# Batch 0's last k tokens as fp32 through two hardware queues, and all sums of phi(k) ahead of v, in a linear-attention + MoE kernel

## The chip, the cores and the metric

The kernel runs on one core of one Trainium2 chip. Its time is device microseconds of one execution; 0.2% of it (about 0.58 us) is the least difference that counts here as a change. The profile is one execution recorded by the hardware profiler: PE is TensorE, DVE is VectorE, ACT is ScalarE, POOL is GpSimd, SP is SyncE. A name such as L212 is line 212 of the kernel before. DMAs can be issued from POOL (a software queue, which can turn fp32 into bf16 on the way) and from SP and ACT (hardware queues, which in this kernel copy without a cast).

## The reference

```python
def _attn_ref(q, k, v):              # (8, 8, 576, 64) = batch, heads, tokens, head_dim
    def phi(x):
        return np.where(x > 0, x, np.exp(x) - 1.0) + 1.0
    q_p, k_p = (phi(q), phi(k))
    kv = np.einsum('bhsd,bhse->bhde', k_p, v)
    z = np.sum(k_p, axis=2)
    num = np.einsum('bhsd,bhde->bhse', q_p, kv)
    den = np.einsum('bhsd,bhd->bhs', q_p, z)[..., None] + 1e-06
    return num / den

def _moe_ref(x, w_in, w_out, beta):  # x: 4608 x 512, w_in: 512 x 2048, w_out: 2048 x 512
    h = x @ w_in
    g = h * (1.0 / (1.0 + np.exp(-beta * h)))
    return g @ w_out
```

The attention output of each batch (576 tokens x 512) is the x of the second part. All tensors are fp32 in memory.

## The kernel before

The order of instructions on every engine is written out by hand (a manual schedule); semaphores between engines follow from the data. Matmuls are in bf16. PE does everything in one long sequence: for batch b it does the "h" phase (x times w_in, then Silu on ACT through `silu`, L467, which leaves g), and the "y" phase (g times w_out, L527), and the attention of batch b+1 is slipped in between these matmuls by the `plan` dictionaries. Phi is made of three instructions: `exp` on ACT, `relu` (max with 0, plus 1) on DVE, and `phi` (the minimum of both) on DVE. The scale by 1/beta is put into w_out by `w_out_scale` (L212 on DVE, L214 on ACT).

Batch 0 has its own code, since nothing can hide it: its 576 tokens are laid out as 64 partitions x 9 tokens (index j) for heads 0 to 3 (g = 0) and again 64 partitions x 9 for heads 4 to 7 (g = 1). Its loads are pieces (`load_nine`, L133, two DMAs each, one for each g): the last four tokens of each nine of k (`k_last`, fp32, j from KF = 5 to 8) by SP; the first five of k, the first four of q, v in two pieces and the rest of q by POOL, with cast; then w_in in four DMAs, w_out, and the next batches, all in POOL's queue. The row of beta comes through ACT's queue and is transposed by PE (`beta_trans`, L193) between two stretches of dummy matmuls (`warm`, L611), which are there while PE has no data.

The start of batch 0, then, in the order of each engine:

- ACT: `exp9` of the first five of k, of `k_last`, of q tokens 0-1 and 2-3 (all L266); the copy of the first transposed q out of PSUM (`q_out9`, L387), half of `kv_evac9` (L387, into `kv_bd`), the second `q_out9`, `exp9` of the rest of q, the copy of x transposed, the load of the Silu table (`silu_table`, L617), the first Silus.
- DVE: `relu9` (L274) of the first k, of `k_last`; `phi9` (L280) of the first k; `relu9` of q; `phi9` of `k_last`; `phi9` of q tokens 0-1 and 2-3; `make_beta` (five small instructions, L199 to L205); the other half of `kv_evac9` (L385); then `num_norm` (L435 to L437) of the first two token pairs.
- PE: `kv_mm0` (L325) four times: the sums of phi(k) over the first five tokens (moving operand: ones), the products with v of these, the sums of the last four, and, after the first `q_trans9` (L293), the products with v of the last four; then the second `q_trans9`, a `warm`, `num_mm` (L421) of the first two token pairs, four `warm`, and the transposes of x (`x_trans`, L455), upon which the h phase begins.

At the end of batch 0's h phase, while PE starts on `y_phase_wide(0)` (L527, four token tiles for each of ff = 0 to 11, then the rest), batch 1 is prepared. ACT takes exp of k (`exp_(1, 1)`) and of q (`exp_(1, 0)`, both L229). DVE takes the two `relu` (L237), `w_out_scale(2)` (four instructions, which wait for the DMAs of that part of w_out into `g`), `phi(1, 1)` for k, `phi(1, 0)` for q (L242), and a copy of v. `w_out_scale(2)` gives the weights of ff = 8 to 11. After ff = 10 PE transposes batch 1's q (`q_trans`, L395), which needs `phi(1, 0)`, and makes `kv_mm(1)` (L362); both take a buffer from the pool of two `att` buffers in PSUM, in this order.

Of the kernel before, what the change touches and what calls it, by code (L numbers as in the profile page):

```python
# [16 lines left out]
def kernel(  # L17
# [73 lines left out]
    def clear_tail(i):  # L91
        nc.vector.memset(xqk[i][TAIL:P, :, :, NJ, :], 0.0)
# [22 lines left out]
    N9 = S // TAIL  # L115

    def nine(a, spec):
# [10 lines left out]
    KF = 5  # L128
    k_last = g_f[:, 0 : HH * (N9 - KF) * D].rearrange(
        "p (h j d) -> p h j d", h=HH, j=N9 - KF  # L130
    )

    def load_nine(dst, src, j0, j1, eng=nc.gpsimd):  # L133
        for g in range(2):
            eng.dma_start(  # L135
                out=dst[g * TAIL : (g + 1) * TAIL].rearrange("p h j d -> p h (j d)"),
                in_=src[0, g * HH : (g + 1) * HH, :, :]
                .rearrange("h (p j) d -> p h j d", j=N9)[:, :, j0:j1, :]
                .rearrange("p h j d -> p h (j d)"),
            )  # L140

    small = consts.tile([P, 2], F32)
    nc.vector.memset(small, 0.0)
    nc.scalar.activation(small[:, 0:1], small[:, 0:1], ACTF.Exp)
    nc.vector.memset(g_sb[0][:, FC - 1, :], 0.0)  # L145
    load_nine(k_last, k, KF, N9, eng=nc.sync)
    clear_tail(1)
    nc.vector.memset(vraw[1][TAIL:P, :, NJ, :], 0.0)
    beta_row = consts.tile([FC, P], F32)
    nc.scalar.dma_start(out=beta_row, in_=moe_beta.rearrange("(c p) -> c p", p=P))  # L150

    identity = consts.tile([P, P], BF16)
    ident16 = consts.tile([FC, FC], F32)
# [37 lines left out]
    def beta_trans():  # L191
        st["bps"] = mm_bank([P, 512])[:, 0:FC]
        nc.tensor.matmul(  # L193
            st["bps"], beta_row, ident16, is_transpose=True, start=True, stop=True
        )
# [11 lines left out]
    def w_out_scale(i, on_dve=4):  # L207
        for c in range(4):
            ff = 4 * i + c
            dst, src, by = w_out_sb[i][:, c, :], w_out_f[i][c // 2][:, c % 2, :], rbeta[:, ff : ff + 1]  # L210
            if c < on_dve:
                nc.vector.tensor_scalar(dst, src, by, None, ALU.mult)  # L212
            else:
                nc.scalar.activation(dst, src, ACTF.Copy, scale=by)  # L214


    st = {}
# [16 lines left out]
    def relu(b, a, h0=0, h1=H):  # L234
        if h0 == 0:
            st[b, "r", a] = work.tile([P, H, NT, D], BF16, tag="r", name="r")
        nc.vector.tensor_scalar(  # L237
            st[b, "r", a][:, h0:h1], xqk[b % NX][:, a, h0:h1], 0.0, 1.0, ALU.max, ALU.add
        )

    def phi(b, a, h0=0, h1=H):
        nc.vector.tensor_tensor(  # L242
            st[b, "p"][:, a].rearrange("p j (h d) -> p h j d", h=H)[:, h0:h1],
            st[b, "r", a][:, h0:h1], st[b, "e", a][:, h0:h1], ALU.min,
        )
# [9 lines left out]
    def work9(tag, **kw):  # L255
        return nine(work.tile([P, H, NT, D], BF16, tag=tag, name=tag, **kw), "jhd")

    def in9(a, j0, j1):
        if a == 1 and j0 >= KF:
            return k_last[:, :, j0 - KF : j1 - KF]  # L260
        return x9[a][:, :, j0:j1]

    def exp9(a, j0, j1):
        if j0 == 0:
            st["e9", a] = work9("e", bufs=3)
        nc.scalar.activation(  # L266
            st["e9", a][:, j0:j1].rearrange("p j h d -> p h j d"), in9(a, j0, j1),
            ACTF.Exp,
        )

    def relu9(a, j0, j1):
        if j0 == 0:
            st["r9", a] = work9("r")
        nc.vector.tensor_scalar(  # L274
            st["r9", a][:, j0:j1].rearrange("p j h d -> p h j d"), in9(a, j0, j1),
            0.0, 1.0, ALU.max, ALU.add,
        )

    def phi9(a, j0, j1):
        nc.vector.tensor_tensor(  # L280
            st["p9"][a][:, j0:j1], st["r9", a][:, j0:j1], st["e9", a][:, j0:j1],
            ALU.min,
        )
# [29 lines left out]
    def kv_cols(kvp, g, a):  # L313
        m0 = a * 2 * (D + 1)
        return kvp[g][:, m0 : m0 + 2 * (D + 1)].rearrange("p (i e) -> p i e", i=2)

    def kv_mm0(kvp, j0, j1, of_v):


        for j in range(j0, j1):  # L320
            for a in range(2):
                for g in range(2):
                    gs = slice(g * TAIL, (g + 1) * TAIL)
                    cols = kv_cols(kvp, g, a)
                    nc.tensor.matmul(  # L325
                        cols[:, :, 0:D] if of_v else cols[:, :, D],
                        st["p9"][1][gs, j, 2 * a : 2 * a + 2, :],
                        v9[gs, 2 * a : 2 * a + 2, j, :] if of_v else ones[gs],
                        start=(j == 0 and a == 0 and not of_v),
                        stop=(j == N9 - 1 and a == 1 and of_v),  # L330
                        skip_group_check=True,
                    )
# [17 lines left out]
        )  # L350


    def kv_mm(b, p0=0, p1=KC):


        kvp = att_banks()[:, 0, 0 : KC * (D + 1)].rearrange("p (c e) -> p c e", c=KC)
        st[b, "kvp"] = kvp
        for p in range(p0, p1):
            for j in range(NT):
                for g in range(2):  # L360
                    c0 = p * P + g * D
                    nc.tensor.matmul(  # L362
                        kvp[g * D : (g + 1) * D, p, :],
                        st[b, "p"][:, 1, j, c0 : c0 + D],
                        vaug[b % 2][:, j, 2 * p + g, 0 : D + 1],
                        start=(j == 0), stop=(j == NT - 1), skip_group_check=True,
                    )
# [114 lines left out]
    def h_phase(b, x, groups, plan):  # L482
        for i, (ff, t0, t1) in enumerate(groups):
            hp = mm_bank([P, 512])
            h_mm(b, x, hp, ff, t0, t1)
            silu(b, ff, hp, t0 * P, t1 * P)
            run(plan, i)
# [121 lines left out]
    def warm(n):  # L609
        for _ in range(n):  # L610
            nc.tensor.matmul(  # L611
                st["warm"], g_sb[0][:, FC - 1, 0:P], g_sb[0][:, FC - 1, :],
                start=True, stop=True, skip_group_check=True,
            )
# [4 lines left out]
    def F(f, *a, **k):  # L619
        return lambda: f(*a, **k)  # L620
# [3 lines left out]
    warm(10)  # L624
    beta_trans()
    warm(15)
    exp9(1, 0, KF)
    exp9(1, KF, N9)
    exp9(0, 0, 2)
    exp9(0, 2, QF)  # L630
    relu9(1, 0, KF)
    relu9(1, KF, N9)
    phi9(1, 0, KF)
    relu9(0, 0, QF)
    phi9(1, KF, N9)
    phi9(0, 0, 2)
    phi9(0, 2, QF)
    make_beta()
    kvp = [mm_bank([P, 512]) for _ in range(2)]
    kv_mm0(kvp, 0, KF, False)  # L640
    kv_mm0(kvp, 0, KF, True)
    kv_mm0(kvp, KF, N9, False)
    qb = att_banks(BF16)
    q_trans9(0, qb, 0)
    q_out9(0, 1, qb, 0, False)
# [9 lines left out]
    num_norm(0, 1)  # L655
    exp9(0, QF, N9)
    relu9(0, QF, N9)
    warm(4)
    x_trans(0, 0)
    silu_table()  # L660
    x_trans(0, 1, dve=True)
# [13 lines left out]
    def q_rest():  # L675
        for t in range(2, NT):
            q_trans9(t, qb2, (t - 2) * 256)
        for t in range(2, NT):
# [24 lines left out]
    silu_table()  # L703
    relu(1, 1)
    relu(1, 0)
    w_out_scale(2)
    phi(1, 1)
    phi(1, 0)
    v_copy(1, 0, HH)
    v_copy(1, HH, H, dve=False)  # L710
    y_phase_wide(0, {
        4: [F(load_next, 3)],
        10: [
            F(q_trans, 1, 0, 1, 2, 3), F(kv_mm, 1), F(kv_evac, 1), F(w_out_scale, 3, 2),
        ],
        11: [F(num_mm, 1, 0), F(num_norm, 1, 0)],
        12: [F(num_mm, 1, 1), F(num_norm, 1, 1), F(x_trans, 1, 0, wide=True)],
# [20 lines left out]
    silu_table()  # L738
    y_phase_wide(1, {
        1: [F(phi, 2, 0), F(q_trans_dma, 2), F(phi, 2, 1)],  # L740
        6: [F(kv_mm, 2), F(kv_evac, 2)],
        8: [F(num_mm, 2, 0), F(num_norm, 2, 0)],
        9: [F(num_mm, 2, 1), F(num_norm, 2, 1)],
        10: [F(num_mm, 2, 2), F(num_norm, 2, 2)],
# [3 lines left out]
    for b in range(2, B + 1):  # L748
        n = b + 1
        groups = ALL  # L750
        plan = {}
        if b == 2:
            groups = (
                [(ff, 0, 2) for ff in range(8)] + [(ff, 2, 4) for ff in range(8)] + ALL[8:]
            )
        o = len(groups) - FC
        if n < B:
            plan[3 + o] = [F(relu, n, 0), F(phi, n, 0), F(q_trans_dma, n)]
            plan[5 + o] = [F(relu, n, 1), F(phi, n, 1)]
            plan[7 + o] = [F(v_copy, n), F(held_v, b + 3, n)]  # L760
            plan[12 + o] = [F(kv_mm, n)]
            plan[13 + o] = [F(kv_evac, n)]
        h_phase(b, xT[b % 3] if b < B else xT_tail, groups, plan)
        plan = {}
        if n + 1 < B:
            begin(n + 1)
            exp_(n + 1, 1)
            exp_(n + 1, 0)
        if n < B:
            for t in range(NT if n % 2 else NJ):  # L770
                plan[1 + 2 * t] = [F(num_mm, n, t)]
                plan[2 + 2 * t] = [F(num_norm, n, t)]
            plan[12] = [F(held_kq, b + 3, n)]
        y_phase(b, plan)
# [30 lines left out]
```

## Time and profile before

| | us |
|---|---|
| median of 5 runs (lowest, highest) | 291.71 (291.61, 291.73) |
| the profiled execution's own time | 291.72 |
| its span, first to last instruction | 289.8 |
| PE busy (97% of the span) | 281.5 |
| ACT busy (60%) | 174.0 |
| DVE busy (41%) | 118.0 |
| POOL busy (19%) | 53.8 |
| mean granted TensorE clock | 0.998 |

The profiled execution is 1.9 us longer than its span; that is time around the program which this change has no part in. PE is busy nearly always, so what matters is where it is not: the waits of PE, the stretch from 0 to 16 us in which its busy time is mostly `warm`, and the chain that leads to each wait. Times in the timeline are from the span's start. A timeline line can merge several instructions; "x4" at its end is their number, and the second column is the time from the first's start to the last's end. In square brackets stands the idle time before it and what ended it.

### The profile page before, as it was taken

How to read it: one execution, taken by the hardware profiler on the slowest of the kernel's cores; microseconds unless marked ns; L12 is line 12 of the kernel's file. 1: busy time of each engine (PE TensorE's matmuls, PEld its weight loads, DVE VectorE, ACT ScalarE, POOL GpSimd, SP SyncE). 2: the span in 40 equal slices, each digit the busy share in tenths (PEclk: the TensorE clock that was granted, in tenths of full speed). 3: DMA queues.
4: the chain of work that ended last, by engine and by line, in shares of the span. 5: the costliest groups of instructions: out<-in, count | busy, mean ns of one | idle time of the engine just before them, and what ended most of it. 6: DMA issues, size and time to landing. Idle time of an engine off the chain costs nothing.

```text
span 289.8 us, 4740 instructions
## 1 busy us (share of the span) xinstructions
PE 281.5 (97%) x1895; PEld 143.0 (49%) x1895; DVE 118.0 (41%) x235; ACT 174.0 (60%) x232; POOL 53.8 (19%) x79
## 2 busy tenths in 40 slices
PE   8889999999999999999999999999999999999994
PEld 3466445644576444454445444554455444444443
DVE  3874387504670365326532655173517300110012
ACT  2888788889998843875277617771850086017500
POOL 8923574300051204020402040000000000000000
PEclk9999999999999999999999999999999999999999
DMA  8999999999379977975794889333503500120033
GB/s 146 200 207 345 256 276 193 257 167 157 62 209 183 131 143 114 208 100 143 120 214 53 160 106 189 72 98 107 102 2 91 111 36 0 67 81 0 0 74 74
DMA packets 75766, 38.07 MB, mean 131 GB/s; under 512 B 43344, under 2 KB 70240, under 8 KB 75744
## 3 DMA queue, kind: packets, MB, share of 16 engines
q0 software_dynamic: 38912, 20.19, 49.0%
q1 hardware_dynamic: 36640, 17.44, 26.1%
q8 instruction: 15, 0.25, 0.4%
q10 hardware_dynamic: 192, 0.14, 0.2%
q14 instruction: 7, 0.06, 0.1%
HBM read 36.71 MB, written 9.44 MB: 159 GB/s over the span
## 4 chain that ended last, share of the span: by engine, by line
PE 83%; DMA 9%; POOL 4%; DVE 1%; ACT 1%; issue 1%; POOLq 0%; DVEq 0%
PE mm L527 38%; PE mm L475 37%; DMA xqk<-in_moe_w_out_dram 5%; DMA g<-in_moe_w_out_dram 4%; PE att L421 3%; PE att L362 2%; POOL xqk L135 1%; PE mm L558 1%; PE att L475 1%; POOL w_in L162 1%; DVE qk_p L242 1%; POOL vraw L135 1%; ACT q_pT L387 1%; PE att L395 0%; DVE w_out L212 0%
## 5 line engine op out<-in xcount | busy, mean ns | idle before, releaser
L467 ACT ACTIVATE g<-mm,beta_c 128x512 bf16<-128x512 f32 (+2 forms) x160 | 97.7, 623 | 86.2 <-PE mm L475 86.1
L527 PE MATMUL mm<-w_out,g 128*128 128x512 bf16 x560 | 128.0, 379 | 0.0
L475 PE MATMUL mm<-xT,w_in 128*128 128x512 bf16 (+2 forms) x576 | 107.5, 344 | 0.1
L475 PEld LDWEIGHTS <-w_in 128*128 128x128 bf16 x672 | 63.8, 98 | 59.4 <-DVE xT L385 0.4
L527 PEld LDWEIGHTS <-g 128*128 128x128 bf16 x560 | 53.1, 98 | 59.0 <-issue 0.3
L537 DVE COPY y_sb<-mm 128x512 f32<-128x512 f32 x27 | 18.7, 691 | 72.9 <-PE mm L527 69.4
L229 ACT ACTIVATE e<-xqk 128x2560 bf16<-128x2560 bf16 x14 | 31.9, 2329 | 0.1
L242 DVE TENSOR_TENSOR qk_p<-r,e 128x2560 bf16<-128x2560 bf16 x14 | 20.8, 1489 | 12.8 <-ACT e L229 12.2
L437 DVE TENSOR_TENSOR xs<-att,rden 128x512 bf16<-128x512 f32 x36 | 24.9, 691 | 1.2
L372 DVE CAST kv_bd<-att 64x260 bf16<-64x260 f32 x14 | 6.0, 427 | 35.9 <-PE att L362 35.8
L435 DVE TENSOR_SCALAR den<-att 128x8 f32<-128x8 f32 x36 | 5.8, 162 | 26.6 <-PE att L421 26.6
L421 PEld LDWEIGHTS <-q_pT 128*128 128x128 bf16 (+1 forms) x160 | 10.9, 100 | 9.5 <-issue 1.7
L421 PE MATMUL att<-kv_bd,q_pT 128*128 128x130 bf16 (+1 forms) x160 | 14.2, 222 | 0.7 <-DVE kv_bd L385 0.4
L475 PE MATMUL mm<-xT_tail,w_in 128*128 128x512 bf16 x64 | 14.0, 379 | 0.0
L594 POOL COPY held<-xT 1x1 bf16<-1x1 bf16 x4 | 2.0, 510 | 63.9 <-DMA xT<-xs 63.9
L237 DVE TENSOR_SCALAR r<-xqk 128x2560 bf16<-128x2560 bf16 x14 | 12.1, 871 | 3.9 <-DMA xqk<-in_q_dram 2.4
L611 PE MATMUL mm<-g 128*128 128x512 bf16 x30 | 9.1, 457 | 1.2 <-DVE g L145 1.2
L229 ACT ACT_TABLE_LOAD x7 | 9.0, 1283 | 0.1
L72 POOL DMA_DIRECT2D vraw<-in_v_dram x7 | 6.4, 910 | 9.6 <-DVE vaug L385 4.5
L72 POOL DMA_DIRECT2D xqk<-in_k_dram x7 | 7.1, 1021 | 4.5 <-DMA w_in<-in_moe_w_in_dram 1.6
L436 DVE RECIPROCAL rden<-den 128x8 f32<-128x8 f32 x36 | 7.3, 203 | 1.2
L475 PE MATMUL att<-xT,w_in 128*128 128x512 bf16 x32 | 7.2, 379 | 0.0
(77 smaller groups left out, 136.6 us busy)
## 6 DMA issues: line engine op xcount, KB each, us to landing
out_dram<-y_sb SPq DMA_DIRECT2D x28, 256.0 KB, 2.3
xqk<-in_k_dram POOLq DMA_DIRECT2D x7, 512.0 KB, 8.7
xqk<-in_q_dram POOLq DMA_DIRECT2D x7, 512.0 KB, 10.8
vraw<-in_v_dram POOLq DMA_DIRECT2D x7, 512.0 KB, 11.7
w_in<-in_moe_w_in_dram POOLq DMA_DIRECT2D x4, 512.0 KB, 10.2
g<-in_moe_w_out_dram POOLq DMA_DIRECT2D x4, 512.0 KB, 10.7
out_dram<-y_sb SPq DMA_DIRECT2D x14, 128.0 KB, 5.2
xqk<-in_moe_w_out_dram POOLq DMA_DIRECT2D x2, 512.0 KB, 14.3
```

The lines of the kernel that those rows point to most:

```text
L72: eng.dma_start(out=dst[:, :, 0:NJ, :].rearrange("p h j d -> p h (j d)"), in_=src[b, :, 0:MAIN, :].rearrange("h (p j) d -> p h (j d)", j=NJ),)
L229: nc.scalar.activation(st[b, "e", a][:, h0:h1], xqk[b % NX][:, a, h0:h1], ACTF.Exp)
L237: nc.vector.tensor_scalar(st[b, "r", a][:, h0:h1], xqk[b % NX][:, a, h0:h1], 0.0, 1.0, ALU.max, ALU.add)
L242: nc.vector.tensor_tensor(st[b, "p"][:, a].rearrange("p j (h d) -> p h j d", h=H)[:, h0:h1], st[b, "r", a][:, h0:h1], st[b, "e", a][:, h0: ...
L421: nc.tensor.matmul(nps[r0 : r0 + n, p // 2, c0 : c0 + 2 * (D + 1)], st[bb, "qT"][:, t, p, :n], kv_bd[bb % 2][:, p], start=True, stop=True, ...
L436: nc.vector.reciprocal(rden[:n], den[:n])
L437: nc.vector.tensor_mul(xs[:n], nv[:, :, :, 0:D], rden[:n, :, :, None].to_broadcast([n, 2, 4, D]))
L467: nc.scalar.activation(g_sb[b % 2][:, ff, c0:c1], hp[:, c0:c1], ACTF.Silu, scale=beta_c[:, ff : ff + 1],)
L475: nc.tensor.matmul(hp[:, c0:c1], w_in_sb[ff // 4][:, kc, (ff % 4) * P : (ff % 4 + 1) * P], x[:, t0:t1, kc, :] if b < B else x[:, kc, c0:c1 ...
L527: nc.tensor.matmul(yp, g_sb[b % 2][:, ff, t * P : (t + 1) * P], w_out_sb[ff // 4][:, ff % 4, :], start=(ff == 0), stop=(ff == FC - 1),)
L537: nc.vector.tensor_copy(y_sb, yp)
L611: nc.tensor.matmul(st["warm"], g_sb[0][:, FC - 1, 0:P], g_sb[0][:, FC - 1, :], start=True, stop=True, skip_group_check=True,)
```

## The change

Half of `k_last` (g = 0) is loaded by SP and half (g = 1) by ACT, both as the first thing that these engines do, ahead of ACT's load of the Exp table; beta's row goes to SP's queue, behind SP's half. On ACT and on DVE, `k_last` is worked on first: its exp, relu and phi stand ahead of those of the first five tokens of k. On PE the sums of phi(k) over all nine tokens are one run of 36 matmuls, ahead of all products with v. Two of the four `warm` between `num_mm` and the transposes of x are taken out. In the preparation of batch 1, `phi(1, 1)` stands ahead of `w_out_scale(2)` on DVE. The PSUM buffer of `kv_mm` is taken by a function of its own, `kv_bank`, which for batch 1 stands ahead of `q_trans`; for the other batches the order stays what it was.

```diff
-    def load_nine(dst, src, j0, j1, eng=nc.gpsimd):
-        for g in range(2):
+    def load_nine(dst, src, j0, j1, engs=(nc.gpsimd, nc.gpsimd)):
+        for g, eng in enumerate(engs):
             eng.dma_start(
...
     small = consts.tile([P, 2], F32)
+    load_nine(k_last, k, KF, N9, engs=(nc.sync, nc.scalar))
     nc.vector.memset(small, 0.0)
     nc.scalar.activation(small[:, 0:1], small[:, 0:1], ACTF.Exp)
     nc.vector.memset(g_sb[0][:, FC - 1, :], 0.0)
-    load_nine(k_last, k, KF, N9, eng=nc.sync)
...
-    nc.scalar.dma_start(out=beta_row, in_=moe_beta.rearrange("(c p) -> c p", p=P))
+    nc.sync.dma_start(out=beta_row, in_=moe_beta.rearrange("(c p) -> c p", p=P))
...
-    def kv_mm(b, p0=0, p1=KC):
-        kvp = att_banks()[:, 0, 0 : KC * (D + 1)].rearrange("p (c e) -> p c e", c=KC)
-        st[b, "kvp"] = kvp
-        for p in range(p0, p1):
+    def kv_bank(b):
+        st[b, "kvp"] = att_banks()[:, 0, 0 : KC * (D + 1)].rearrange(
+            "p (c e) -> p c e", c=KC
+        )
+
+    def kv_mm(b):
+        kvp = st[b, "kvp"]
+        for p in range(KC):
...
     warm(15)
+    exp9(1, KF, N9)
     exp9(1, 0, KF)
-    exp9(1, KF, N9)
     exp9(0, 0, 2)
     exp9(0, 2, QF)
+    relu9(1, KF, N9)
+    phi9(1, KF, N9)
     relu9(1, 0, KF)
-    relu9(1, KF, N9)
     phi9(1, 0, KF)
     relu9(0, 0, QF)
-    phi9(1, KF, N9)
     phi9(0, 0, 2)
     phi9(0, 2, QF)
     make_beta()
     kvp = [mm_bank([P, 512]) for _ in range(2)]
-    kv_mm0(kvp, 0, KF, False)
+    kv_mm0(kvp, 0, N9, False)
     kv_mm0(kvp, 0, KF, True)
-    kv_mm0(kvp, KF, N9, False)
     qb = att_banks(BF16)
     q_trans9(0, qb, 0)
...
-    warm(4)
+    warm(2)
     x_trans(0, 0)
...
     relu(1, 0)
+    phi(1, 1)
     w_out_scale(2)
-    phi(1, 1)
     phi(1, 0)
...
-            F(q_trans, 1, 0, 1, 2, 3), F(kv_mm, 1), F(kv_evac, 1), F(w_out_scale, 3, 2),
+            F(kv_bank, 1), F(q_trans, 1, 0, 1, 2, 3), F(kv_mm, 1), F(kv_evac, 1), F(w_out_scale, 3, 2),
```

More of the change, by code (lines that the diff above doesn't have):

```diff
@@ L263, in exp9 @@
     def exp9(a, j0, j1):
-        if j0 == 0:
+        if ("e9", a) not in st:
             st["e9", a] = work9("e", bufs=3)
@@ L271, in relu9 @@
     def relu9(a, j0, j1):
-        if j0 == 0:
+        if ("r9", a) not in st:
             st["r9", a] = work9("r")
@@ L740 @@
         1: [F(phi, 2, 0), F(q_trans_dma, 2), F(phi, 2, 1)],
-        6: [F(kv_mm, 2), F(kv_evac, 2)],
+        6: [F(kv_bank, 2), F(kv_mm, 2), F(kv_evac, 2)],
         8: [F(num_mm, 2, 0), F(num_norm, 2, 0)],
@@ L760 @@
             plan[7 + o] = [F(v_copy, n), F(held_v, b + 3, n)]
-            plan[12 + o] = [F(kv_mm, n)]
+            plan[12 + o] = [F(kv_bank, n), F(kv_mm, n)]
             plan[13 + o] = [F(kv_evac, n)]
```

## The prediction

> **What bounds the kernel now.** I first read the chain that ended last. From 46 us to the end it is PE alone, matmul after matmul; ahead of that it hangs on a DMA, DVE and ACT. Columns are start, length, what.
>
> ```profile
> 27.45 11.04 DMA g<-in_moe_w_out_dram
> ...
> 39.15 0.77 DVE w_out L212
> 39.92 2.81 DVE qk_p L242 x2
> 42.72 0.05 issue
> 42.77 1.08 PE att L395 x16
> 43.87 1.95 ACT q_pT L387 x2
> ```
>
> So the last place at which something other than PE decides is batch 1's `phi(1, 0)`: what starts `q_trans` earlier at 42.77 ends the kernel earlier by as much, unless it meets another limit. The waits of PE (total us, times, longest) say the same:
>
> ```profile
> PE mm L325 <- DVE qk_p L280: 0.7, 1, 0.7
> PE att L395 <- DVE qk_p L242: 0.7, 1, 0.7
> PE mm L455 <- DVE xs L437: 0.6, 1, 0.6
> PE att L421 <- DVE kv_bd L385: 0.4, 1, 0.4
> PE att L421 <- ACT q_pT L387: 0.3, 1, 0.3
> ```
>
> All waits at the start matter only if PE arrives at 42 us later through them and if `phi(1, 0)` comes later too. Third, the timeline of the start, for DVE and PE:
>
> ```profile
> 8.81 0.82 DVE L280 TENSOR_TENSOR qk_p<-r,e 128x1280 bf16<-128x1280 bf16 x1
> 9.55 0.63 DVE L274 TENSOR_SCALAR r<-xqk 128x1024 bf16<-128x1024 bf16 x1
> 10.10 1.34 DVE L280 TENSOR_TENSOR qk_p<-r,e 128x1024 bf16<-128x1024 bf16 x3
> 11.29 0.73 PE L325 MATMUL mm<-vraw,qk_p 64*128 64x128 bf16 x16
> 11.37 0.16 DVE L199 COPY beta_s<-mm 128x16 f32<-128x16 f32 x1
> 12.54 0.54 DVE L385 CAST kv_bd<-mm 64x130 bf16<-64x130 f32 x2
> 13.13 0.63 PE L421 MATMUL att<-kv_bd,q_pT 128*128 128x130 bf16 x8 [0.37 <-DVE kv_bd L385]
> ```
>
> The products are done at 11.29 + 0.73 = 12.02, and ACT's half of `kv_bd` runs from 12.05 to 12.61. DVE's half starts only at 12.54, since DVE is busy with phi and `make_beta`. `num_mm` waits for that half. Fourth, the timeline of ACT and DVE around 37 us:
>
> ```profile
> 35.20 4.57 ACT L229 ACTIVATE e<-xqk 128x2560 bf16<-128x2560 bf16 x2
> 37.23 1.12 DVE L212 TENSOR_SCALAR w_out<-g,rbeta 128x512 bf16<-128x512 f32 x2 [0.31 <-DMA g<-in_moe_w_out_dram]
> 38.52 1.40 DVE L212 TENSOR_SCALAR w_out<-g,rbeta 128x512 bf16<-128x512 f32 x2 [0.17 <-DMA g<-in_moe_w_out_dram]
> 39.84 2.87 DVE L242 TENSOR_TENSOR qk_p<-r,e 128x2560 bf16<-128x2560 bf16 x2
> ```
>
> DVE waits 0.31 + 0.17 us for w_out here and is otherwise busy until 42.71. Last, stretches of the start, with the busy times of the engines, clock, DMA share and GB/s:
>
> ```profile
> 2.00:2.50 0.50, 0.50 (x3) 0.17 (x2) 0.35 (x2) 0.24 (x2) 0.50 (x1) 1.00 0.41 59
> 2.50:3.00 0.50, 0.50 (x3) 0.23 (x2) 0.44 (x2) 0.00 (x0) 0.50 (x2) 1.00 0.69 131
> 3.00:3.50 0.50, 0.50 (x3) 0.22 (x2) 0.43 (x3) 0.00 (x0) 0.50 (x2) 1.00 1.11 345
> ```
>
> **Part 1, the loads.** In narrow windows of the DMA view, SP's two halves of `k_last` land 4.0 and 5.2 us after issues at 0.75 and about 1.46, thus at 4.75 and 6.7; the first k lands at 1.25 + 4.2 = 5.45 and 2.0 + 5.4 = 7.4 (ACT starts on it at 7.51); the last piece of v at 6.5 + 4.9 = 11.4. With both halves issued at 0.75, and rows of 1024 B, 1024 B and 640 B (from the sizes) taken in turn from three queues where two took turns before, `k_last` should be in by about 5.5 to 6.0: an estimate, and at the worst 6.7 as now. The first k lands last either way, and behind the same bytes, so its landing stays near 7.4. It comes earlier by what the second issuer fills of the stretch from 2 to 3 us, where 59 and 131 GB/s moved against 345 right after: at most 0.35 us (some 100 KB at 250 to 345 GB/s), at the least nothing. I call it s and take 0.15, nearer the low end, as POOL's own stream starts no sooner. All of POOL's queue (q, v, w_in, w_out, batch 1) moves by s.
>
> The Trainium skill's page "DMA: Bandwidth & Descriptors" (section "Issuing engines are not separate DMA queues") speaks against such a split: all issuers end on the same engines, and only issue time is saved. By it s would be 0 and the time 0.15 us longer than my sum; no run here has shown which holds.
>
> Beta's row moves behind SP's half: landing 2.6 now (0.92 + 1.7), then about when that half lands, 5.5 to 6. `beta_trans` stands at 5.40 on PE with 15 `warm` queued behind it; they end at 8.97, and PE then waits 0.72 for phi. So up to 0.7 us of delay is covered; without that cover each further us delays the sums of phi(k). ACT's 0.71 us of issuing (SP's duration) and its table load (1.28) end by 2.8, long before 5.5: nothing.
>
> **Part 2, the start.** `k_last` at about 5.8: exp 1.04, relu and phi 0.82 + 0.60 (start to start) end by about 7.6, in time now empty on ACT and DVE. The first k follows as before: exp to 8.78, phi at 8.81, relu of q 9.55. Then DVE skips the 0.60 of phi of `k_last` (10.10 to 10.70), so `make_beta` and the cast come 0.60 earlier: 12.54 becomes 11.94. PE's sums and products take the same time in another order (0.26 + 0.21 of sums, then v, which has landed at 9.9), and the products of the last four still wait for v's landing at 11.3 to 11.4: they end at 12.02. DVE's cast therefore starts at 12.05 and `num_mm` at about 12.65 instead of 13.13: 0.48, plus s. What is late next? q's second transpose, copied by ACT 12.64 to 13.24, only for the second `num_mm`; ACT is free from 14.39, and the x copy would come at 14.70 (15.18 now); w_in's first part lands at 8.31 + 7.3 = 15.6, before the Silu table is loaded (16.6); w_in's second at about 18.4 against a need at 18.95. None takes the 0.48. The two removed `warm` (0.43 us) lie in PE's wait for xs: nothing. From 16 to 42 us PE and ACT are dense (PE busy 25.74 of 26.0), so both arrive 0.48 + s earlier.
>
> **Part 3, the swap on DVE.** exp of k ends at 37.49 now, at 37.01 then. phi(1, 1) at 1.40 ends 38.41. Then four scales, both DMAs (37.2, 38.45) being in. They start 0.40 apart in the first pair and 0.63 to 0.72 apart in the others, which run while POOL issues DMAs (until 39.66). Two at 0.65 and two at 0.40 end at 40.51, phi(1, 0) at 1.47 more: 41.98, against 42.71. All four at 0.40 would be 41.5, all at 0.69 would be 42.64. PE, 0.48 earlier at ff = 8 (38.86), waits 0.2 for its first weights, finishes ff = 10 at about 41.7, so cannot use less than that. Gain at `q_trans`: 0.73, between 0.1 and 1.0, plus s. v of batch 1 (ACT's copy ends 42.94, on a landing at 41.6) is needed only after `q_trans`, 43.0.
>
> `kv_bank`: `num_mm` (45.86, waited 0.30 for ACT's second copy) can start after the kv cast, 45.50. But ff = 15 waits for ACT's last scale, ending 47.03, in both orders, so the 0.3 is given back: nothing; at best 0.1. For other batches nothing moves.
>
> **Sum.** 0.73 + 0.15 = 0.88 us. The profiled execution took 291.72, within 0.01 of the median of 291.71: 290.8.
>
> **Rivals.** (A) The gain is used up on DVE: if `num_mm` isn't earlier (v landing late, or `k_last` landing after 6.7), phi(1, 0) ends at 37.49 + 1.40 + 2.1 to 2.76 + 1.47 = 42.46 to 43.12, against 42.71: 291.4 to 292.1, no change. For it: DVE idles only 0.48 us there, so the swap alone has little to fill. Against: DVE's 0.60 is plainly off the start's path.
> (B) Slower, by the transfers: a third queue costs throughput, so POOL's stream is later. The DMA share is above 1.1 from 3 us on, so there is no spare. From 0.5 us of delay on, v's last piece (11.4) eats the 0.48; at 1 us, exp of k ends 0.5 later than now and phi(1, 0) at 43.0 to 43.6: 292.0 to 292.6, and later if w_in's first part holds the h phase as well. Against: the bytes are the same, and two queues already shared without a drop below 190 GB/s.
> (C) Beta's row lands so late that PE idles well past 6.1, or its clock falls back: the first ten `warm` are 0.427 apart, the 15 later 0.2165. If those ran at 0.427, they would end near 12 instead of 8.97, and the sums 2 us late: 293 or more. The Trainium skill ("TensorE: Matmul & The Clock Gate", Part 1) puts the fall back after an idle window of about 3.4 us; no wait here is that long.
>
> **Chances.** Forecast 0.66 (own range 290.2 to 291.1), A 0.20, B 0.10, C 0.04. Faster by over 0.2% (0.58 us, about what a measurement can tell) 0.66; within 0.20; slower 0.14. The range reaches from s = 0.35 with fast scales (290.2) into A, to 291.9.
>
> **What would show it.** Exp of `k_last` on ACT by 6.2, of the first k at 7.2 to 7.5; `make_beta` at 10.6 to 10.8; `num_mm` at 12.5 to 12.7; no PE wait for `kv_bd` beyond 0.1; first Silu at 16.5 to 16.7; phi(1, 1) on DVE at about 37, ahead of the scales; `q_trans` at about 41.9; then the same PE chain. I am wrong if `num_mm` is at 13 or later, if the first k lands after 7.7, or if `q_trans` starts at 42.6 or later despite an earlier start.

## The result, and the profile after

| | before | after |
|---|---|---|
| median of all runs (lowest, highest), us | 291.67 (291.04, 292.87) of 49 | 292.41 (291.14, 294.6) of 26 |
| the profiled execution, us (its span) | 291.72 (289.8) | 291.98 (290.1) |

The change makes the kernel slower: the ratio is 1.0026, with a 95% interval from 1.0015 to 1.0036. The forecast was 290.8, faster; the measured time is also past the end of the range (291.9). Two things are to be explained: the 0.26 us of the profiled execution, and another 0.43 us by which the median of the runs lies above it. For the second, one number is needed beside each run, its mean granted TensorE clock: five executions of the changed kernel, all between 292.69 and 292.79 us, have a mean of 0.994 where most have 0.997 to 1.0. Without these five the median is 291.87. Nine of the other 21 still took 292.3 to 294.6 us, at means of 0.998 to 1.0; no recorded fall of the clock explains those.

The same views follow, in the same order as before. First the chain that ended last, cut to the start and to the stretch around 43 us (start, length, what):

```profile
8.64 8.59 DMA w_in<-in_moe_w_in_dram
...
33.48 6.91 PE mm L530 x32
40.41 2.75 PE mm L530 x12
44.10 1.95 ACT q_pT L390 x2
```

Before, the chain ran through `w_out`'s DMA, DVE's scale and phi to `q_trans`. These are gone from it. PE's own matmuls now lead up to 43 us, and ahead of them stands the landing of w_in's first part at 17.23. The DVE pair that the change was read to relieve no longer decides; the start does. The waits of PE (total us, times, longest):

```profile
PE mm L193 <- DMA beta_row<-in_moe_beta_dram: 1.7, 1, 1.7
PE mm L614 <- DVE g L146: 1.2, 1, 1.2
PE mm L478 <- DMA w_in<-in_moe_w_in_dram: 0.9, 1, 0.9
PE mm L458 <- DVE xs L440: 0.8, 2, 0.6
PE att L424 <- ACT q_pT L390: 0.5, 2, 0.3
```

Two waits are new, both on a DMA: 1.7 us for beta's row and 0.9 us for w_in. Gone are the 0.7 for phi of k (L280 before), the 0.7 at `q_trans` and the 0.4 for `kv_bd`; the last two are those that the prediction meant to remove, the first was the cover that it counted on. The timeline of the start shows the first new wait and what is queued behind it:

```profile
0.74 0.74 ACTq L135 DMA_DIRECT2D g<-in_k_dram  x1
0.75 0.76 SPq L135 DMA_DIRECT2D g<-in_k_dram  x1
1.57 0.82 SPq L150 DMA_DIRECT2D beta_row<-in_moe_beta_dram  x1
...
6.60 1.06 ACT L266 ACTIVATE e<-g 128x1024 bf16<-128x1024 f32 x1 [3.58 <-DMA g<-in_k_dram]
...
7.39 0.20 PE L193 MATMUL mm<-ident,beta_row 16*128 16x16 f32 x1 [1.72 <-DMA beta_row<-in_moe_beta_dram]
7.53 3.41 PE L614 MATMUL mm<-g 128*128 128x512 bf16 x15
...
9.10 0.83 DVE L280 TENSOR_TENSOR qk_p<-r,e 128x1280 bf16<-128x1280 bf16 x1
...
10.87 0.60 PE L325 MATMUL mm<-ones,qk_p 64*128 64x2 bf16 x36
...
12.02 0.62 PE L325 MATMUL mm<-vraw,qk_p 64*128 64x128 bf16 x16
...
12.67 0.60 DVE L388 CAST kv_bd<-mm 64x130 bf16<-64x130 f32 x2 [0.37 <-PE mm L325]
...
13.32 0.40 PE L424 MATMUL att<-kv_bd,q_pT 128*128 128x130 bf16 x4
```

Beta's row is issued at 1.57 and used at 7.39; `beta_trans` stood at 5.40 before. The 15 `warm` behind it end at 7.53 + 3.41 = 10.94. Phi of the first k is ready at 9.10 + 0.83 = 9.93, so PE is late by about 0.9 us for data that lies there. DVE now waits for PE (0.37 at the cast) where it held PE back before. `num_mm` is at 13.32: 0.67 later than forecast and 0.19 later than before. The next stretch of PE, and DVE and ACT around 40 us:

```profile
17.28 1.07 PE L478 MATMUL mm<-xT,w_in 128*128 128x128 bf16 x16 [0.91 <-DMA w_in<-in_moe_w_in_dram]
```

```profile
36.10 4.56 ACT L229 ACTIVATE e<-xqk 128x2560 bf16<-128x2560 bf16 x2
...
38.47 1.49 DVE L242 TENSOR_TENSOR qk_p<-r,e 128x2560 bf16<-128x2560 bf16 x1 [1.34 <-ACT e L229]
39.88 1.67 DVE L212 TENSOR_SCALAR w_out<-g,rbeta 128x512 bf16<-128x512 f32 x4
...
41.46 1.48 DVE L242 TENSOR_TENSOR qk_p<-r,e 128x2560 bf16<-128x2560 bf16 x1
...
43.00 1.07 PE L398 MATMUL att<-identity,qk_p 128*128 128x128 bf16 x16
```

The h phase starts 1.27 us later than before (17.28 against 16.01). In this execution w_in's landing sets that start: with an earlier beta row PE would only have waited longer for w_in. The first `mm_y` matmul (the first of the y phase, L530) is 0.89 later (33.32 against 32.43), and exp of k on ACT 0.90 later (36.10 against 35.20). `q_trans` is only 0.23 later (43.00 against 42.77), so 0.66 us has been made up on the way. The kernel's end keeps the 0.23 (0.26 in the executions' times). That the swap earned the 0.66 isn't shown: before, PE waited 0.68 for phi at this place, and a start 0.89 later would have used up that wait first (42.77 - 0.68 + 0.89 = 42.98).

### The profile page after: what moved, and what is told of

Its sections match the earlier page's. It is cut to its first block, busy times and chain, and to the rows that moved or that the text cites. A ratio compares the mean times of both kernels' runs of the same rounds, so it can differ in the third digit from the quotient of the medians.

```text
span 290.1 us, 4737 instructions
## 1 busy us (share of the span) xinstructions
PE 280.7 (97%) x1893; PEld 142.6 (49%) x1893; DVE 116.8 (40%) x235; ACT 174.1 (60%) x232; POOL 54.5 (19%) x79
## 4 chain that ended last, share of the span: by engine, by line
PE 92%; DMA 3%; POOL 2%; ACT 1%; issue 0%; DVE 0%; POOLq 0%
PE mm L530 42%; PE mm L478 41%; PE att L424 3%; DMA w_in<-in_moe_w_in_dram 3%; PE att L478 2%; PE att L365 2%; POOL xqk L135 1%; PE mm L561 1%; POOL vraw L135 1%; ACT q_pT L390 1%; PE att L398 0%; PE mm L458 0%; PE att L458 0%; DVE xT L388 0%; PE att L293 0%
## 5 line engine op out<-in xcount | busy, mean ns | idle before, releaser
L530 PE MATMUL mm<-w_out,g 128*128 128x512 bf16 x560 | 128.2, 379 | 0.0
L530 PEld LDWEIGHTS <-g 128*128 128x128 bf16 x560 | 53.1, 98 | 59.1 <-issue 0.6
L72 POOL DMA_DIRECT2D xqk<-in_q_dram x7 | 7.2, 1031 | 3.9 <-ACT w_out L214 2.1
```

What stands on the lines that cost most here:

```text
L72: eng.dma_start(out=dst[:, :, 0:NJ, :].rearrange("p h j d -> p h (j d)"), in_=src[b, :, 0:MAIN, :].rearrange("h (p j) d -> p h (j d)", j=NJ),)
L530: nc.tensor.matmul(yp, g_sb[b % 2][:, ff, t * P : (t + 1) * P], w_out_sb[ff // 4][:, ff % 4, :], start=(ff == 0), stop=(ff == FC - 1),)
```

## The experiments

The theory: beta's row, behind SP's half of `k_last` on SP's queue, holds back PE, costs the start its gain, and by PE's wait brings the clock down in some executions; the swap alone earns something, the split and the order nothing. One rival: the loss is the split itself, through POOL's stream and w_in's landing. Another: it is the order of the start, or the two `warm` taken out. Each expectation was written ahead of its run, with the theories as they stood then. In each comparison the kernel before ran on the same chip, and its median stands second. Intervals are at 95%.

**Beta's queue alone.** The kernel before, and only this:

```diff
-    nc.scalar.dma_start(out=beta_row, in_=moe_beta.rearrange("(c p) -> c p", p=P))
+    nc.sync.dma_start(out=beta_row, in_=moe_beta.rearrange("(c p) -> c p", p=P))
```

> The kernel before with one edit: beta's row on SP's queue, behind both halves of k_last. B: beta lands at 7 to 8, PE idles from 5.4 to then, the 15 warm end at 10.5 to 11.3, num_mm at 13.3 to 13.8; batch 1's phi, which waits for w_out, hides most of it: 291.8 to 292.2 in most executions, with some of 293 to 295. S: PE waits, but time as before, 291.6 to 291.8, with no more scatter than before.

Measured: 292.66 against 291.71 us, ratio 1.0029, from 1.0013 to 1.0046: as much as the whole change (1.0026), and more than the 291.8 to 292.2 expected of most executions. Beta's row stands behind both halves here, so PE waits a little longer than in the change (2.08 against 1.72). The wait of PE, PE's timeline, and stretches of the start (busy times of PE, PEld, DVE, ACT and POOL, then clock, DMA share, GB/s):

```profile
PE mm L193 <- DMA beta_row<-in_moe_beta_dram: 2.1, 1, 2.1
```

```profile
7.89 5.10 PE L611 MATMUL mm<-g 128*128 128x512 bf16 x15
12.92 0.40 PE L325 MATMUL mm<-ones,qk_p 64*128 64x2 bf16 x20
...
44.16 1.06 PE L395 MATMUL att<-identity,qk_p 128*128 128x128 bf16 x16
```

```profile
7.00:9.00 2.00, 1.25 (x7) 0.66 (x8) 1.09 (x2) 1.28 (x2) 1.83 (x4) 1.00 1.38 195
9.00:11.00 2.00, 2.00 (x6) 0.68 (x5) 1.98 (x4) 1.98 (x3) 2.00 (x3) 0.51 1.42 195
11.00:13.00 2.00, 2.00 (x12) 0.70 (x12) 1.32 (x7) 0.00 (x0) 2.00 (x4) 0.64 1.33 202
```

The 15 `warm` take 5.10 us in place of 3.41, since the granted clock is at half from 9.04 to 12.45. The sums start at 12.92 against 9.69 before, `mm_y` 2.23 later (34.66 against 32.43), and `q_trans` at 44.16 against 42.77: without the swap, too, 0.84 of the delay is made up by then. The mean clock of this execution is 0.994, and the working agrees: 3.41 us at half is 1.7 us lost of 291, or 0.006. Seven of its 12 executions have that mean (292.58 to 293.38 us).

**Beta's row first.** The changed kernel with beta's load as the first thing on ACT's queue, ahead of ACT's half:

```diff
...
+    nc.scalar.dma_start(out=beta_row, in_=moe_beta.rearrange("(c p) -> c p", p=P))
     load_nine(k_last, k, KF, N9, engs=(nc.sync, nc.scalar))
...
-    nc.sync.dma_start(out=beta_row, in_=moe_beta.rearrange("(c p) -> c p", p=P))
```

> The changed kernel with beta's row issued first, on ACT's queue, ahead of ACT's half of k_last; SP keeps its half. Theory T (the loads cost the time: beta's row late on PE, POOL's stream later by 0.3 us, the last engine of w_in's first part later still; order and swap are gains): beta lands by 3 us, the 15 warm end at 9.0 instead of 10.9, the sums of phi(k) start at 9.9 instead of 10.87, num_mm at 12.7 to 12.9 instead of 13.32, the h phase as soon as w_in's first part is in (15.8 to 17.2): some 0.3 to 0.5 us less than the changed kernel, 291.8 to 292.1. Rival R1 (k_last ahead of the first k on ACT and DVE costs the time): num_mm at 13.2 or later, no gain, 292.4. Rival R2 (phi(1, 1) ahead of w_out_scale(2) costs the time): start earlier, time as the changed kernel, 292.4.

Measured: 291.61 against 291.75 us, ratio 1.0008 (0.9989 to 1.0027); 291.8 to 292.1 had been expected. The profiled execution took 291.35. PE's timeline:

```profile
5.76 3.41 PE L614 MATMUL mm<-g 128*128 128x512 bf16 x15
9.40 0.60 PE L325 MATMUL mm<-ones,qk_p 64*128 64x2 bf16 x36 [0.23 <-DVE qk_p L280]
...
11.42 0.61 PE L325 MATMUL mm<-vraw,qk_p 64*128 64x128 bf16 x15 [0.46 <-DMA vraw<-in_v_dram]
...
12.68 0.39 PE L424 MATMUL att<-kv_bd,q_pT 128*128 128x130 bf16 x4 [0.21 <-DVE kv_bd L388]
```

`num_mm` is at 12.68, where the prediction put it (12.65). In the median the loss of the change is gone, though the split, the order and the two missing `warm` are all still in; the interval is too wide to say so by itself, as it reaches 1.0027. But the time isn't 290.8. PE still waits 0.5 for w_in, h starts at 16.26 (16.01 before), and `q_trans` at 42.20. Eight of twelve executions have a median of 291.43; the other four, at a mean clock of 0.994 or less, took 292.52 to 294.31.

**Beta's transpose behind the warm-up.** The changed kernel, beta's row loaded as it is there, but its transpose put behind all 25 `warm`:

```diff
-    warm(10)
+    warm(25)
     beta_trans()
-    warm(15)
```

> The changed kernel with one edit on PE: the transpose of beta's row behind all 25 warm instead of between the first 10 and the last 15; beta stays on SP's queue and lands at 7.3 as before. Theory B (the change lost by beta's row: PE stands still from 5.5 to 7.4, the 15 warm end 2 us later, and in some executions the clock stays at or falls to half in or after that gap): the warm end near 9.0, no execution above 293, the sums start when phi of the first k is done, 9.9, and the median is 291.4 to 291.8, as with beta first. Rival S (the change lost by the split of k_last over two queues, which makes POOL's stream and w_in's first part later): h phase at 16.7 to 17.2 whatever beta does, median 292.2 to 292.5.

Measured: 291.65 against 291.71 us, ratio 1.0002 (0.9989 to 1.0015). Beta's row lands at 6.98, about as late as in the change (7.3), and nobody waits for it: `beta_trans` at 9.48, sums at 9.64, `num_mm` at 12.88, `q_trans` at 42.30. So it is the wait of PE that costs, not beta's transfer. With the two runs above this speaks for the theory against both rivals: beta's wait alone costs as much as the change, and the split, the order and the missing `warm`, together and without that wait, give about the time of before. A part of the loss may still be the rivals': this interval ends at 1.0015, where that of the change begins.

**The change once more,** unedited, for a second profile.

> The changed kernel as it is, beside the three others on one chip. Theory B (PE's idle time behind beta's row is the loss, in two sizes: the 2 us in which the warm start later, and one stretch of 3.4 us at half clock in some executions): median 292.2 to 292.8, with executions at a mean clock of 0.994 lying 0.8 to 1.2 us above those at 0.997 and more. If the loss was particular to the first chip: 291.4 to 291.8.

Measured: 292.32 against 291.55 us, ratio 1.0033 (1.0012 to 1.0053). This time the profile caught an execution with a fallen clock (292.47 us, mean 0.994). The four executions with a mean below 0.996 have a median some 0.7 us above that of the others; 0.8 to 1.2 had been expected. PE's timeline:

```profile
6.92 0.20 PE L193 MATMUL mm<-ident,beta_row 16*128 16x16 f32 x1 [1.97 <-DMA beta_row<-in_moe_beta_dram]
7.05 5.10 PE L614 MATMUL mm<-g 128*128 128x512 bf16 x15
12.08 0.60 PE L325 MATMUL mm<-ones,qk_p 64*128 64x2 bf16 x36
...
14.53 0.40 PE L424 MATMUL att<-kv_bd,q_pT 128*128 128x130 bf16 x4
```

The clock is at half from 7.48 to 10.90, and `num_mm` comes 1.21 us later than in the first profile of the change, although beta's row came 0.47 earlier. PE doesn't wait for w_in any more, since it now arrives after it (h at 17.42); `mm_y` starts at 33.83 and `q_trans` at 43.51. The two profiles are two ways of being late: w_in where the clock stays up, the clock where it falls.

**The loads of before under the orders of after.** The changed kernel with `k_last` on SP alone and beta's row on ACT again.

```diff
-    load_nine(k_last, k, KF, N9, engs=(nc.sync, nc.scalar))
     nc.vector.memset(small, 0.0)
...
+    load_nine(k_last, k, KF, N9, engs=(nc.sync, nc.sync))
...
-    nc.sync.dma_start(out=beta_row, in_=moe_beta.rearrange("(c p) -> c p", p=P))
+    nc.scalar.dma_start(out=beta_row, in_=moe_beta.rearrange("(c p) -> c p", p=P))
```

> The changed kernel with the loads as before: both halves of k_last on SP, beta's row on ACT, at their old places; all changes of order kept. T: k_last at 6.7, the sums at 9.8, num_mm at 12.7, w_in's first part at 15.6, the h phase at 15.7, q_trans of batch 1 at 42.1: 290.8 to 291.1, clearly under the kernel before. R1: num_mm at 13.1 or later and 291.7 or more. R2: start 0.4 us earlier, but 291.7 or more.

Measured: 291.70 against 291.75 us, ratio 1.0001 (0.9988 to 1.0014); 290.8 to 291.1 had been expected, a miss. The last half of `k_last` lands near 7.1 here (exp at 7.12), and as it is now first on ACT, everything behind it moves: PE waits 1.34 for phi at 10.29.

```profile
10.29 0.60 PE L325 MATMUL mm<-ones,qk_p 64*128 64x2 bf16 x36 [1.34 <-DVE qk_p L280]
...
13.03 1.27 PE L424 MATMUL att<-kv_bd,q_pT 128*128 128x130 bf16 x8
```

The clock is at half from 11.92 to 15.33, after a wait of only 1.34 us. So the order of the change is no better than the later half of `k_last` lets it be.

**The order of the start alone.** The kernel before with the order of the start, two `warm` less and `kv_bank`, but its own loads and no swap: the change's own diff from `exp9` to `warm(2)`, and `kv_bank`. Its core:

```diff
     warm(15)
+    exp9(1, KF, N9)
     exp9(1, 0, KF)
-    exp9(1, KF, N9)
...
-    kv_mm0(kvp, 0, KF, False)
+    kv_mm0(kvp, 0, N9, False)
     kv_mm0(kvp, 0, KF, True)
-    kv_mm0(kvp, KF, N9, False)
...
-    warm(4)
+    warm(2)
```

> The kernel before with the changed order of batch 0's start (k_last first on ACT and DVE, all sums ahead of v, two warm fewer) and kv_bank, but with the loads of before and without the swap on DVE. T: num_mm at 12.7 and the h phase 0.3 to 0.4 us earlier, but batch 1's phi waits behind w_out_scale(2), whose DMA lands at 38.45 whatever PE does: q_trans at 42.7, time as before, 291.6 to 291.8. R1: num_mm at 13.1 or later, 291.7 to 292.4. If R2 is true (the swap is the loss), this one is the fastest of the four, 291.2 or less.

Measured: 291.87 against 291.75 us, ratio 0.9997 (0.9985 to 1.0009): no gain, but by another way than expected. `num_mm` was to be at 12.7 and was at 13.32, since PE had the last pieces of v only at 12.06 in this execution (a wait of 0.81), and `q_trans` then still waits 0.52 for phi as in before (42.80). Even an earlier start could not have shown here, since phi held `q_trans`; and this start isn't earlier.

**The split alone,** with beta's row first on ACT, as in the second experiment, and all orders of before.

```diff
...
+    nc.scalar.dma_start(out=beta_row, in_=moe_beta.rearrange("(c p) -> c p", p=P))
+    load_nine(k_last, k, KF, N9, engs=(nc.sync, nc.scalar))
     nc.vector.memset(small, 0.0)
...
-    load_nine(k_last, k, KF, N9, eng=nc.sync)
...
-    nc.scalar.dma_start(out=beta_row, in_=moe_beta.rearrange("(c p) -> c p", p=P))
```

> The kernel before with k_last split over SP and ACT as in the change, but beta's row first on ACT's queue; all orders of work as before. B: k_last at 5.5 to 6.5, POOL's first k and all behind it 0.1 to 0.3 later, hidden behind DVE: 291.6 to 291.9. S: the first k at 7.7 or later, w_in's first part at 15.8 or later, 292.0 to 292.4.

Measured: 291.97 against 291.71 us, ratio 1.0007 (0.9997 to 1.0017): no gain, perhaps a loss; the interval doesn't decide. The first k is in use at 7.98 (7.51 before), the pieces of v hold PE twice, `num_mm` is at 13.57 and `q_trans` at 43.32. A load that isn't used earlier bought nothing here.

**The swap alone.** The kernel before and only this:

```diff
-    w_out_scale(2)
     phi(1, 1)
+    w_out_scale(2)
     phi(1, 0)
```

> The kernel before with one edit: phi(1, 1) ahead of w_out_scale(2). T: phi(1, 1) from 37.5 to 38.9, four scales at 0.40 to 0.65 each to 40.6 to 41.0, phi(1, 0) ends at 42.1 to 42.5 instead of 42.71, q_trans at 42.2 to 42.5 instead of 42.77: 291.1 to 291.5. R2: PE waits for its weights at ff = 8 or phi(1, 0) ends at 42.7 to 43.1: 291.7 to 292.1.

Measured: 291.33 against 291.75 us, ratio 0.9990, from 0.9981 to 0.9999; 291.1 to 291.5 had been expected. DVE and PE:

```profile
37.56 1.49 DVE L242 TENSOR_TENSOR qk_p<-r,e 128x2560 bf16<-128x2560 bf16 x1 [0.33 <-ACT e L229]
38.97 2.04 DVE L212 TENSOR_SCALAR w_out<-g,rbeta 128x512 bf16<-128x512 f32 x4
...
40.93 1.48 DVE L242 TENSOR_TENSOR qk_p<-r,e 128x2560 bf16<-128x2560 bf16 x1
...
42.46 0.90 PEld L395 LDWEIGHTS <-qk_p 128*128 128x128 bf16 x16 [0.62 <-DVE qk_p L242]
```

`q_trans` is at 42.46, 0.31 earlier: DVE has filled its idle time between the scales with phi(1, 1), which is all it had (0.31 + 0.17). PE's weight load still waits 0.62 there. This version has the lowest median of the study, and its interval excludes 1, if narrowly. But 0.42 us in the medians is less than the 0.58 us that counts here as a change, this is one interval of twelve, and the three kernels below that hold the swap too, with other edits, measured 0.9994, 1.0002 and 0.9995, each with 1 inside its interval. So that the swap pays by itself is likely, and not shown.

**The swap with an earlier start by other means.** The swap, and `make_beta` on DVE put ahead of the first relu, where DVE is idle, so that it is out of the way of the `kv_bd` cast.

```diff
+    make_beta()
     relu9(1, 0, KF)
...
-    make_beta()
```

> A candidate for a version that beats both: the kernel before with the swap of phi(1, 1) and w_out_scale(2), and make_beta moved on DVE ahead of the first relu, into time in which DVE is empty (3.9 to 7.5); loads and all else as before. If DVE's half of kv_bd is what held num_mm: make_beta at 5.7 to 7.0, the cast at 12.05 instead of 12.54, num_mm at 12.6, the h phase at 15.6 to 15.8, q_trans of batch 1 at 42.0 to 42.2: 290.8 to 291.1. If the start is held by something else (v's landing, w_in's first part): as with the swap alone, 291.3.

Measured: 291.56 against 291.71 us, ratio 0.9994 (0.9985 to 1.0004); 290.8 to 291.1 had been expected, again a miss of the same kind. The `kv_bd` cast comes at 12.34 instead of 12.54 and `num_mm` at 12.99, but PE then waits for w_in:

```profile
16.95 1.07 PE L475 MATMUL mm<-xT,w_in 128*128 128x128 bf16 x16 [0.92 <-DMA w_in<-in_moe_w_in_dram]
```

With none of the change's loads in it, the h phase is 0.94 us later than in before's profile. The landing of w_in's first part swings from execution to execution: by the packet records its last DMA engine is done between 15.2 and 16.7 us in the fourteen profiles of this study.

**Warm-ups.** Three more, to see whether more `warm` keeps the clock up: the swap with 17 in place of 15 `warm` behind `beta_trans`; the same with `make_beta` early; and the kernel with beta's row first, with the two `warm` back ahead of `x_trans` (`warm(4)`).

```diff
-    warm(15)
+    warm(17)
```

```diff
-    warm(2)
+    warm(4)
     x_trans(0, 0)
```

> The kernel before with the swap on DVE, and 17 warm instead of 15 in the second stretch, which fill 0.43 us of the 0.7 us in which PE waits for phi. If it is idle time of PE ahead of the sums that lets the clock fall: median 291.2 to 291.4 as with the swap alone, and at most 2 of 12 executions below a mean clock of 0.996. If the fall has another cause: as many as in the kernel before (a third) and 291.4 to 291.6.

> The last candidate: the kernel before with the swap, make_beta ahead of the first relu on DVE, and 17 warm. If w_in's first part (15.2 to 16.7 by run) is what the start ends on, make_beta's move gives nothing beyond the swap: 291.2 to 291.4. If DVE's cast still decided in some executions: 290.9 to 291.2.

> The changed kernel with beta's row first on ACT's queue, and with four warm instead of two ahead of the transposes of x. If the two removed warm cost clock (4 of 12 executions without them were at 0.991 to 0.994, and took 292.5 to 294.3): fewer low ones, and a median of 291.2 to 291.5. If they are idle filling that nothing needs: 291.5 to 291.7 and as many low ones.

Measured, against 291.55 for before: 291.47 (ratio 1.0002, 0.9986 to 1.0017), 291.48 (0.9995, 0.9982 to 1.0007) and 291.75 (1.0006, 0.9998 to 1.0015). None has a lower ratio than the swap alone (0.9990). In each of the three only one execution of 11 or 12 has a mean clock below 0.996; with beta's row first and `warm(2)` there were 4 of 12. Whether the extra `warm` keeps the clock up these few executions don't decide; the swap alone has 2 of 11 without it. If it does, the 0.43 us of two more `warm` ahead of the sums, or w_in (PE waits 1.3 in the second of them, 0.8 in the third), would take back what that gives.

## Why the prediction was wrong, point by point

**Beta's row (Part 1): the step that failed.** The prediction gave a landing at 5.5 to 6 and a cover of 0.72. The cover was right: PE's old wait for phi is gone, and what isn't covered went on to the sums, 10.87 for 9.69. The landing was mis-sized: 5.7 us after an issue at 1.57, so 7.3, for a transfer of 8 KB that took 1.7 on ACT's empty queue. The delay of `beta_trans` was 2.0 us (5.40 to 7.39) against a cover of 0.72. The prediction's own rows held the warning: SP's second half landed 5.2 us after its issue in before, so a row behind a half would have landed at 6.8 by that row, past the 6.1 that rival C named. By itself the move of the row measured 1.0029, and the change without PE's wait for it 1.0002.

```profile
xqk<-in_k_dram POOLq DMA_DIRECT2D x2, 160.0 KB, 5.7
g<-in_k_dram ACTq DMA_DIRECT2D x1, 256.0 KB, 4.4
g<-in_k_dram SPq DMA_DIRECT2D x1, 256.0 KB, 5.8
beta_row<-in_moe_beta_dram SPq DMA_DIRECT2D x1, 8.0 KB, 5.7
```

These are the first DMA issues of the changed kernel, with KB each and median us from issue to landing. SP's half and the row behind it land 5.8 and 5.7 us after their issues.

**The clock (rival C).** It was given 0.04, on the ground that no wait would be as long as an idle window of 3.4 us, the figure that the Trainium skill ("TensorE: Matmul & The Clock Gate", Part 1) gives for the fall to half. The runs differ from that reading: the clock fell after waits of 2.08 (beta's queue alone), 1.97 (the change's second profile) and 1.34 us (loads of before, with small matmuls around it). It stayed up after 1.72 us in the change's first profile. What agrees is the length: each of the three recorded stretches at half lasts 3.41 us, the length of the window that the page names, and the page says that this window runs freely, whatever the kernel does. The clock records of all fourteen profiles bear that out: every stretch at full clock, from one change to the next, is a whole number of times 3.413 us (83 in nine profiles, 84 in two; 82, 82, and 2 and 80 in the three where the clock fell), and the first rise lies between 4.07 and 6.92 us. The 3.41 us ahead of a fall hold the wait and some work: 2.08 us of waiting in 5.63 to 9.04 (61%), 1.97 in 4.07 to 7.48 (58%), and 1.34 in 8.50 to 11.92 (39%, with the small matmuls of the sums behind it). In the change's first profile PE was idle for 1.71 us, 50%, of the window from 5.67 to 9.08, and the clock stayed up. So the place of the window has a part in which execution falls, and the plain share of idle time doesn't decide it; what does wasn't tested.

The fall isn't peculiar to the change. In the three sessions 12 of 35, 12 of 35 and 8 of 35 executions of the kernel before have a mean clock below 0.996, against 5 of 26 and 4 of 12 of the change; no profile shows where before's falls lie. So these counts don't show that beta's wait makes the fall more frequent. A fall costs more in the change, though: between the medians above and below 0.996 lie 0.7 to 0.9 us there, and 0.2 to 0.5 in before. Rival C's mechanism, beta's row so late that PE idles and the clock falls back, is the one that happened, in a part of the executions; its price of 293 or more was a little too high even for those (292.69 to 292.79), since I had all 15 `warm` at half the clock and a part of them ran at full.

**s, the earlier stream (Part 1): it didn't come.** I took 0.15 from the second issuer. The stretches of the changed kernel that were to be filled:

```profile
2.00:2.50 0.50, 0.50 (x3) 0.17 (x2) 0.35 (x2) 0.50 (x1) 0.50 (x1) 1.00 0.61 43
2.50:3.00 0.50, 0.50 (x3) 0.22 (x2) 0.44 (x2) 0.49 (x2) 0.50 (x2) 1.00 0.83 115
3.00:3.50 0.50, 0.50 (x3) 0.21 (x2) 0.43 (x3) 0.01 (x1) 0.50 (x2) 1.00 0.56 121
```

From 2 to 3.5 us, 43, 115 and 121 GB/s moved, against 59, 131 and 345 before. By the packet records ACT's half moved from 2.27 to 4.3 and SP's from 3.64 to 5.5, nearly one after the other, and POOL's first data moved at 4.46 instead of 3.30. From 6.5 us on, by bytes, POOL's stream is 0.3 us behind before's in this profile. That s is a loss is not shown by it: the first 1.1 MB of POOL's stream are in at 10.52 us here and at 10.39 and 10.42 in the two other profiles with these loads, at 10.14, 10.15 and 10.37 in the three with the split and beta's row first (POOL's first data at 3.1 to 3.3 there), and between 10.19 and 10.48 in the seven with the loads of before. The last of `k_last` landed at 6.51, near the worst end that I had named (6.7); in the two other profiles with these loads it landed at 5.89 and 6.08, about as estimated. The Trainium skill's rule against such a split ("DMA: Bandwidth & Descriptors", "Issuing engines are not separate DMA queues") was nearer than my sum: by it s is 0, and the split alone measured 1.0007 (0.9997 to 1.0017), no gain.

**The start (Part 2).** DVE's 0.60 came off the start's path as worked out, and the cast waited for PE, not PE for the cast; with beta out of the way `num_mm` was at 12.68 for 12.65. "None takes the 0.48" failed: w_in's first part takes it. I let it land at 15.6 from one profile. In the change it was issued at 8.64 for 8.31, as POOL's issues were later, and landed at 17.2; in the kernel with beta's row first PE waited 0.5 for it. In the late case one 16 KB packet of instructions, some 0.95 us long, is the only entry of another queue between 14 and 16 us; but before's profile has such a packet at 14.82 and w_in landed at 15.57 there, so that it caused the delay is not shown. A landing that ends 0.4 us ahead of its need in one profile and swings over 1.5 us is no cover. The two `warm` were put down at nothing, and the medians agree (291.61 with two and 291.75 with four, in different sessions); whether they narrow the spread, 4 of 12 executions against 1 of 11 at a lower clock don't decide.

**The swap (Part 3).** Right in mechanism, and in sign as far as the runs tell. Its gain of 0.73 at `q_trans` held an earlier exp (0.48) that didn't come. Alone it gave 0.31 in the profile and 0.42 in the medians, between the ends of 0.1 and 1.0. What it gave in the changed kernel is open, since no run has the change without it. With the swap, PE's arrival and phi(1, 0) are level at `q_trans`: phi(1, 0) ends 0.06 us ahead of it in each profile below (42.94, 43.45 and 42.14), and both hang on the start. With the swap and the new start, `mm_y` starts 9.7 to 9.9 us ahead of `q_trans` in each profile (33.32 to 43.00, 33.83 to 43.51, 32.30 to 42.20), and in before that distance is 9.66 without PE's wait (32.43 to 42.77, less 0.68). So time lost at the start now costs nearly its full price at the end (0.51 us for 0.51 between the two profiles of the change), where the kernel before had 0.68 us of PE's wait for phi to hide it. That fits with before losing less by a fallen clock (medians of 291.67 and 291.91 us above and below a mean of 0.996, 23 and 12 executions of one session) than the swapped start with beta first (291.43 and 292.9).

**`kv_bank`.** Nothing was forecast and nothing came, but not by the stated way: `num_mm` of batch 1 still waits 0.30 for ACT's second copy in the changed kernel (46.09), so there was no 0.3 to be given back.

**Rivals A and B.** A (the gain used up, 291.4 to 292.1) holds the kernels without beta's wait, by w_in's landing rather than by v's. B has POOL's stream 0.5 to 1 us late; it was 0.3 late in one profile and within before's swing in the others.

**Left open.** Five executions of the change took 294.2 to 294.7 us, some 2 us longer yet; four of them show a mean clock of 1.0 and one 0.994. A first rise of the clock that comes one window late would fit, but no profile caught one. A mean of 1.0 doesn't speak against it, since the mean counts no loss ahead of the first rise: the profile of "beta's transpose behind the warm-up" has a mean of 1.000 though its clock rose only at 6.83 us, with its `warm` 0.43 us apart until then. The executions of the change between 292.3 and 293.5 us at means of 0.998 and more are open as well. Why the two hardware queues' packets went one after the other, and which went first (ACT's in the change, SP's in the kernel with beta's row first), is open too.

## What to carry to other kernels

Price a moved DMA by its new place in a queue and not by its size, and look at which in-order engine stands behind it: an 8 KB row moved behind a 256 KB half landed 5.7 us after its issue in place of 1.7, and the engine that waited for it had 15 instructions and the whole start queued behind that wait. Before a gain is counted, ask of each landing that lies just ahead of its need how much it swings; 0.4 us of slack in one profile was no slack. When two parts of a kernel hide each other's waits, remove them one at a time and measure each: here one swapped line alone had a lower median than the kernel with all the rest.

## What the runs showed of the hardware

- TensorE's granted clock fell to half for 3.41 us after waits of 1.3 to 2.1 us in the first 12 us of three profiles, and stayed up after waits of 1.7, 1.3 and 1.2 us in three others; of the change it fell in one profile and not in the other; 15 matmuls of 128x512 then took 5.10 instead of 3.41 us. In all fourteen profiles the clock changed only at whole multiples of 3.413 us from its first rise, which came between 4.07 and 6.92 us.
- Two halves of 256 KB, issued at 0.74 and 0.75 us on two hardware queues, moved at 2.27 to 4.3 and 3.64 to 5.5 us, and the first data of POOL's queue came 1.16 us later than before (4.46 for 3.30). With an 8 KB load ahead of the half on the second queue, POOL's first data came at 3.1 to 3.3 (three profiles).
- An 8 KB load landed 1.6 to 1.7 us after its issue on an empty queue and 5.2 to 5.7 us after it behind one or two halves of 256 KB.
- DVE's scales of w_out from fp32 to bf16 started 0.40 us apart once POOL had nothing to issue (four in 1.67 us in the change), against 0.63 to 0.72 beside POOL's DMA issues before. It isn't always so: with beta's queue alone, three of the four overlapped POOL's issues and took 0.48 to 0.49 us each, as without them.
